# Local attention with a PReLU feed-forward: banks, first loads, visits, conversion pieces and shared sums rearranged

## The chip, the cores and the metric

The kernel runs on one core of a Trainium2 chip. The metric is the device time of one execution in microseconds (us), lower is better; several runs are timed and their median is given. The program is one launch. Its engines work side by side, each through its own list of instructions in order: TensorE (matmuls, PE in the profile; its weight loads are PEld), VectorE (DVE), ScalarE (ACT), GpSimd (POOL) and SyncE (SP), which here only issues DMA transfers. GpSimd and ScalarE can issue transfers as well.

## What is computed

Local attention over chunks of 64 positions, 8 heads of 64 columns, is followed by a feed-forward layer whose activation has a slope of its own for every hidden column where the input is negative.

```python
q_c, k_c, v_c = (a.reshape(B, H, nc, 64, D) for a in (q, k, v))      # 8 x 8 x 9 chunks, D = 64
scores = (1 / sqrt(D)) * matmul(q_c, k_c.transpose(0, 1, 2, 4, 3))
scores = scores - max(scores, axis=-1)
attn = exp(scores); attn = attn / (sum(attn, axis=-1) + 1e-9)
x = matmul(attn, v_c) -> (4608 tokens, 512)
h = x @ w_in                                                          # 512 -> 2048
g = maximum(h, 0) + alpha * minimum(h, 0)
out = g @ w_out                                                       # 2048 -> 512
```

## The kernel before

The 4608 tokens are 36 sub-blocks of 128 tokens (two chunks of 64 each); four sub-blocks are a block of 512 tokens, nine blocks in all. Float32 products are made of three passes of rounded matmuls: every operand is split into a high part (a copy on ACT) and a low part (a subtraction on DVE).

**Blocks 0 to 2 (plain).** The list `steps` has 48 steps, numbered `n`. One step is one 128-column slice `f` of the hidden layer for one block: `ffn_in` (L317, 12 matmuls of 512 columns into a bank of `ps_h`, of which there are two), `prelu` (L307 and L308 on ACT, L309 on DVE), the split into `gh` and `gl` (L329 on ACT, L330 on DVE), and one or two steps later `ffn_out` through `second` (L341, 12 matmuls into the four banks `ps_o0` to `ps_o3`, which hold a block's results). Steps 0 to 2 are block 0, 3 to 11 block 1, 12 to 24 block 0 again, 25 to 31 block 1 again, 32 to 47 block 2. The weights of slice `f` are loaded by SP (`fetch`) and converted on DVE and ACT (`split_weight`, L130 to L138) one step after the other; the conversion of slices 2, 3 and 4 is held until the x of sub-blocks 4, 6 and 7 is made.

**Attention of sub-blocks 0 to 7 (early).** Each goes through three stages, `attend(0)` scores and softmax, `attend(1)` transposes (L248) and two copies (L255, L256), `attend(2)` values (L266) and the split into `xh` and `xl` (L298, L299). Sub-blocks 0 to 3 come before the steps; 4 to 7 are spread over the steps 0 and 1 (`beside`). `attn_psum` picks the bank: scores always use `ps_a` (two banks); the transposes and values of sub-blocks 0 to 3 use `ps_o`, those of 4 to 7 `ps_a`. All first loads are issued by SP, in the order `q0 k0 wi0 q1 k1 v0 wo0 q2 k2 v1 ...`.

**Attention from sub-block 8 on.** A `visit` makes the values of one sub-block (L278, from the transposed probabilities `pT`) and the scores of the one two further on (L200, from `q_sb` and `k_sb`, one buffer each), then the softmax, the copies of x (L303 on ACT and L304 on DVE for block 2, L294 on ACT for later blocks), and `attn_blocks`, which transposes 32 by 32 squares on DVE (L231) and has SP issue eight small transfers `pT <- t` (L238). The list `visits` says ahead of which step each of the first 14 is made; the sixth makes the values of sub-block 11, the last of block 2. `combine` (in the steps listed in `COMBINE`) prepares sums of weights on DVE for what follows and is put behind the last softmax.

**Blocks 3 to 8 (three pairs).** A pair's products are made with seven instead of eight block products (`ORDERS` gives their order). `convert` makes 14 pieces of operands of a pair from x (a subtraction L567 or L571 for eight of them, and a split, L549 and L550); for the first pair they are made during steps 40 to 47, ahead of the step's `ffn_in`. `first_product` (L593) has eight parts `j`; `second_product` (L705) runs over seven products `i`, each with eight parts `j`. Weights stream through a ring of four 512 KB buffers: when a unit is used up, `stream` has GpSimd issue the load of the one four units on (L531, `raw<-wo_a` and its like). The results are `y11`, `y12`, `y21`, `y22`; products that several results share are added by GpSimd's accumulating transfers (L712, L724, L730) of 512 KB each, and the results leave by SP (`done`, L681). In `second_product` these transfers stand at `(i, j)` = (3, 0), (3, 5) and (4, 2), and after the products 7 and 5.

The order on each engine comes from a planner. It takes the instructions in program order as priorities, raised inside `tc.high_priority`, and puts on each engine the first one that its own model of time holds ready. From step 20 on the matmuls keep their program order (`pe`). `tc.issue_after(ins)` puts what its block makes behind `ins` on that instruction's engine. The names in the profile are those of the buffers: early `q`, `k`, `v` and probabilities live in buffers called `wi` and `wo`, the y tiles in `xh` and `xl`.

Of the kernel before, what the change touches and what calls it, by code (L numbers as in the profile page):

```python
# [12 lines left out]
ALU = mybir.AluOpType  # L13
# [14 lines left out]
def tile_local_attention_prelu_ffn(  # L28
# [12 lines left out]
    nc = tc.nc  # L41
# [113 lines left out]
    def attn_load(s, parts="qkv"):  # L155
        early = s < EARLY
        if "q" in parts:
            q_sb = qs[s // 2 % 2][:, s % 2] if early else load.tile([P, H, C], F32, name="q_sb")
            kb = kbds[s % NBD] if early else load.tile([P, H, C], F32, name="k_sb")
            nc.sync.dma_start(out=q_sb, in_=qT[:, s].rearrange("p (h t) -> p h t", t=C))  # L160
            if not early:
                nc.sync.dma_start(out=kb, in_=kT[:, s].rearrange("p (h t) -> p h t", t=C))
            for c in range(2 if early else 0):
                rows = slice(c * C, (c + 1) * C)
                nc.sync.dma_start(out=kb[rows, c], in_=kT[rows, s].rearrange("p (h t) -> p h t", t=C))
            qkv[s] = [q_sb, kb, None]
        if "v" in parts:
            v_sb = vs[s // 2 % 2][:, s % 2] if early else load.tile([P, DM], F32, name="v_sb", bufs=2)
            loads.append(nc.sync.dma_start(out=v_sb, in_=v[s * P:(s + 1) * P, :]))
            qkv[s][2] = v_sb  # L170

    def attn_psum(s, n):
        if s < SPB and n:
            t = 2 * (s % 2) + n - 1
            return ps_o.tile([P, 512], F32, name=f"ps_o{t}")
        return ps_a.tile([P, 512], F32, name="ps_a")
# [134 lines left out]
    def ffn_in(x, f):  # L311
# [15 lines left out]
        with tc.high_priority(offset=HIGH):  # L327
            prelu(g, hps, f)
            nc.scalar.copy(gh, g)  # L329
            nc.vector.tensor_tensor(gl, g, f32(gh), op=ALU.subtract)  # L330
# [84 lines left out]
    attn_load(0, "q")  # L415
    fetch("wi", 0)
    attn_load(1, "q")
    attn_load(0, "v")
    fetch("wo", 0)
    attn_load(2, "q")  # L420
    attn_load(1, "v")
    attn_load(3, "q")
# [21 lines left out]
    visits = [21, 23, 25, 27, 29, 31, 33, 35, 37, 39, 41, 42, 44, 45]  # L444
# [220 lines left out]
    def second_product(g, b, operands, conversion, end):  # L665
# [11 lines left out]
        def done(ys, half, col):  # L677
            for m in range(2):
                rows = slice((2 * half + m) * P, (2 * half + m + 1) * P)
                cols = slice((b - PLAIN + col) * TB, (b - PLAIN + col + 1) * TB)  # L680
                nc.sync.dma_start(out=outT[rows, cols], in_=ys[:, m])  # L681

        kept = None
        for i in ORDERS["wo"]:
# [8 lines left out]

            shared = {(3, 0): y22, (3, 5): y21, (4, 2): y12}
            for j in range(JF):
# [14 lines left out]
                if (i, j) in shared:  # L710
                    ys = shared[i, j]
                    nc.gpsimd.dma_start(out=ys, in_=y11, accum_op=ALU.add)  # L712
                    if ys is y22:
                        done(y22, 1, 1)
                    elif ys is y12:
                        done(y12, 0, 1)
# [5 lines left out]
            elif i == 7:  # L722
                copy(y21, ps)
                nc.gpsimd.dma_start(out=y22, in_=y21)  # L724
            elif i == 2:
                add(y11, ps)
                done(y11, 0, 0)
            elif i == 5:
                copy(y12, ps)
                nc.gpsimd.dma_start(out=y22, in_=y12, accum_op=ALU.add)  # L730
            elif i == 3:
                add(y12, ps)
            elif i == 6:
                copy(y11, ps)
            else:
                add(y21, ps)
                done(y21, 1, 0)
# [8 lines left out]
    for n, (p, b, f) in enumerate(steps):  # L746
# [34 lines left out]
        if n >= len(steps) - 8:  # L781
            for _ in range(1 if len(conversion) > 10 else 0 if n < len(steps) - 3 else 4):
                if conversion:
                    conversion.pop(0)()
        pending.append((acc, ffn_in(x[b], f), f, f0, f1, b, False))

        if len(pending) > (1 if n < 20 else 2):
            second(*pending.pop(0))
    assert not combined and not conversion and not finals
# [62 lines left out]
```

## Time and profile before

| | |
|---|---|
| median of 3 runs | 864.72 us (861.14 to 866.14) |
| the profiled execution | 862.12 us, its span 860.3 us |
| instructions | 15340 |
| TensorE | busy 95%, mean granted clock 0.986 of 2.4 GHz |
| DVE, ACT, POOL | busy 78%, 63%, 23% |
| DMA | 192.39 MB, mean 224 GB/s |

The profile is of one execution. The span runs from its first to its last instruction; times in it count from the span's start. A wait in brackets is idle time of that engine, with what ended it.

### The profile page before, as it was taken

Reading aid. Unit: us, or ns where it says so; the run is one execution under the profiler, and the core shown is the slowest. Engines: PE = TensorE matmul, PEld = TensorE weight load, DVE = VectorE, ACT = ScalarE, POOL = GpSimd, SP = SyncE. Lnnn points to the kernel's source line nnn. Section 1 sums busy time; section 2 is a strip of 40 time slices with the busy share of each in tenths; the row PEclk is TensorE's granted clock in tenths of the full one; section 3 lists DMA queues with packets and bytes.
Section 4 is the critical chain, followed back from the end, with each engine's and each line's share of the span. In section 5 each row is a group of like instructions: output and inputs, shape, how many; then the busy total and the mean of one; then the engine's idle time right before and its main releaser. Section 6 shows DMA issues by size and latency. Waiting matters only on the chain.

```text
span 860.3 us, 15340 instructions
## 1 busy us (share of the span) xinstructions
PE 814.4 (95%) x5248; PEld 648.0 (75%) x5248; DVE 673.3 (78%) x1267; ACT 544.9 (63%) x1392; POOL 200.1 (23%) x324
## 2 busy tenths in 40 slices
PE   4697999999989998999989999999999999999997
PEld 4576888778767776777767877777887788888885
DVE  6769999997997987476768995776789956568874
ACT  6785666667576676487776563877765546556552
POOL 3005222224443420011111221111122221111230
PEclk9899999999999999999999999999999999999999
DMA  9618768637778676587774788877567885555686
GB/s 283 194 50 312 249 199 291 218 129 204 234 247 230 212 232 211 180 260 253 250 261 164 237 220 286 274 253 242 188 200 233 230 297 185 186 193 190 236 218 213
DMA packets 73164, 192.39 MB, mean 224 GB/s; under 512 B 11648, under 2 KB 18816, under 8 KB 72960
## 3 DMA queue, kind: packets, MB, share of 16 engines
q0 software_dynamic: 36464, 127.42, 46.2%
q1 hardware_dynamic: 36480, 63.99, 23.3%
q8 instruction: 42, 0.69, 0.3%
q14 instruction: 34, 0.28, 0.1%
q10 hardware_dynamic: 144, 0.01, 0.0%
HBM read 135.27 MB, written 42.99 MB: 207 GB/s over the span
## 4 chain that ended last, share of the span: by engine, by line
PE 69%; DMA 11%; DVE 6%; issue 4%; ACT 4%; SPq 3%; POOL 2%; DVEq 0%; POOLq 0%; ACTq 0%
PE ps_o L593 18%; PE ps_h L705 12%; PE ps_h L317 10%; PE ps_o L341 9%; PE ps_h L593 8%; PE ps_o L705 8%; DMA raw<-wo_a 3%; SPq L238 2%; DMA pT<-t 2%; ACT pr L220 1%; PE ps_a L278 1%; DMA wi_a<-raw 1%; PE ps_a L200 1%; DMA v_sb<-v 1%; DMA k_sb<-kT 1%
## 5 line engine op out<-in xcount | busy, mean ns | idle before, releaser
L317 PE MATMUL ps_h<-xh,wi 128*128 128x512 f32 x384 | 110.3, 412 | 10.9 <-DVE g L309 5.4
L341 PE MATMUL ps_o<-wo,gh 128*128 128x512 f32 x384 | 114.1, 396 | 0.0
L317 PEld LDWEIGHTS ps_h<-xh,wi 128*128 128x128 f32 x384 | 73.3, 195 | 30.0 <-DVE g L309 6.3
L341 PEld LDWEIGHTS ps_o<-wo,gh 128*128 128x128 f32 x384 | 72.3, 189 | 17.4 <-issue 0.2
L220 ACT ACTIVATE pr<-ps_a,mx 128x64 f32<-128x64 f32 x224 | 67.1, 326 | 28.7 <-DVE mx L217 28.7
L341 PE MATMUL ps_o<-wo,gl 128*128 128x512 f32 x192 | 69.0, 395 | 0.0
L593 PE MATMUL ps_o<-wi,raw 128*128 128x512 f32 x171 | 67.9, 397 | 0.3 <-ACT g L614 0.3
L593 PE MATMUL ps_o<-wo,raw 128*128 128x512 f32 x171 | 67.8, 397 | 0.0
L317 PE MATMUL ps_h<-xl,wi 128*128 128x512 f32 x192 | 54.5, 405 | 0.0
L220 ACT ACTIVATION_READ_ACCUMULATOR pr<-ps_a,mx 128x1 f32 x224 | 48.8, 218 | 0.0
L531 POOL DMA_DIRECT2D raw<-wi_a x42 | 22.4, 534 | 110.8 <-PE ps_o L593 61.6
L307 ACT ACTIVATE g<-ps_h 128x512 f32<-128x512 f32 x48 | 29.4, 613 | 29.1 <-PE ps_h L317 24.4
L307 ACT ACTIVATE wo<-gh 128x512 f32<-128x512 f32 x24 | 15.2, 634 | 51.3 <-DVE gh L616 51.3
L549 ACT CAST gh<-wi 128x512 fp32r<-128x512 f32 x48 | 29.9, 623 | 27.5 <-PE ps_o L705 13.1
L329 ACT CAST gh<-g 128x512 fp32r<-128x512 f32 x48 | 29.9, 623 | 26.1 <-DVE g L309 21.3
L317 PEld LDWEIGHTS ps_h<-xl,wi 128*128 128x128 f32 x192 | 37.1, 194 | 9.2 <-DVE xl L304 0.4
L341 PEld LDWEIGHTS ps_o<-wo,gl 128*128 128x128 f32 x192 | 36.2, 189 | 8.7
L531 POOL DMA_DIRECT2D raw<-wo_a x42 | 22.5, 535 | 86.6 <-PE ps_o L705 45.2
L309 DVE SCALAR_TENSOR_TENSOR g<-ps_h,g 128x512 f32<-128x512 f32 x48 | 32.7, 684 | 9.4 <-ACT g L308 9.2
L593 PE MATMUL ps_o<-wi,wo 128*128 128x512 f32 x99 | 39.4, 398 | 0.3 <-ACT g L614 0.3
L593 PE MATMUL ps_o<-wo,wo 128*128 128x512 f32 x99 | 39.1, 395 | 0.0
L330 DVE TENSOR_TENSOR gl<-g,gh 128x512 fp32r<-128x512 f32 x48 | 32.9, 686 | 7.8 <-ACT gh L329 6.6
(249 smaller groups left out, 2269.4 us busy)
## 6 DMA issues: line engine op xcount, KB each, us to landing
raw<-wi_a POOLq DMA_DIRECT2D x42, 512.0 KB, 4.6
raw<-wo_a POOLq DMA_DIRECT2D x42, 512.0 KB, 4.6
wi<-wi_a POOLq DMA_DIRECT2D x21, 512.0 KB, 4.7
wo<-wi_a POOLq DMA_DIRECT2D x21, 512.0 KB, 4.7
wi<-wo_a POOLq DMA_DIRECT2D x21, 512.0 KB, 4.5
wo<-wo_a POOLq DMA_DIRECT2D x21, 512.0 KB, 4.8
k_sb<-kT SPq DMA_DIRECT2D x28, 256.0 KB, 5.0
q_sb<-qT SPq DMA_DIRECT2D x28, 256.0 KB, 4.0
```

The source lines that it names most:

```text
L220: last = nc.scalar.activation(pr[:, g], one, AF.Exp, bias=mx[:, g], scale=SCALE, accum_out=sm[:, g])
L238: nc.sync.dma_start(out=pT[dst, i].rearrange("p h t -> p (h t)"), in_=tb[src, j].rearrange("p h t -> p (h t)"),)
L307: nc.scalar.activation(g, h, AF.Relu, scale=-1.0)
L309: nc.vector.scalar_tensor_tensor(g, in0=h, scalar=0.0, in1=g, op0=ALU.max, op1=ALU.subtract)
L317: pe(nc.tensor.matmul(hps, lhsT=wi[f][:, l, k * P:(k + 1) * P], rhs=xx[:, k], start=(i == 0 and k == 0), stop=(i == 2 and k == NK - 1),))
L329: nc.scalar.copy(gh, g)
L330: nc.vector.tensor_tensor(gl, g, f32(gh), op=ALU.subtract)
L341: pe(nc.tensor.matmul(o, lhsT=a[:, ts], rhs=wo[f][:, l], start=(f == first and i == 0), stop=(f == last and i == 2),))
L531: nc.gpsimd.dma_start(out=f32(t), in_=units[side][n])
L549: hi = nc.scalar.copy(t_hi, t)
L593: pe(nc.tensor.matmul(ps, lhsT=w[:, l, k * P:(k + 1) * P], rhs=xx[:, xl], start=first and at == 0, stop=at == n - 1, skip_group_check=not ...
L705: pe(nc.tensor.matmul(ps[m], lhsT=w[:, l, m * P:(m + 1) * P], rhs=xx, start=i != 6 and j == 0 and n == 0, stop=j == JF - 1 and n == 2, ski ...
```

## The change

Five things. (1) `attn_load` can take a second queue: `q0` and the second half of `k0` are issued by ACT; `q1` and `k1` go ahead of `wi0`, and `wo0` goes behind `v1`. (2) `attn_psum`: sub-blocks 4 and 5 put their transposes and values into `ps_o`, as 0 to 3 do. (3) `visits`: from the sixth on each is one step earlier. (4) The pieces of the first pair: four at steps 40 to 43 as before; of the other ten, three each at steps 45, 46 and 47, issued after `ffn_in` and, on DVE, after the split of the step before, and one after the loop. (5) `second_product`: the shared sums are ten transfers of 256 KB instead of five of 512 KB, and the results leave in 256 KB pieces as their sum is done; a table `sums` says at which `(i, j)` each is written in the program.

```diff
--- before.py
+++ after.py
@@ -152,17 +152,18 @@
     stages = {}
     pdiag = {}
 
-    def attn_load(s, parts="qkv"):
+    def attn_load(s, parts="qkv", other=None):
         early = s < EARLY
         if "q" in parts:
             q_sb = qs[s // 2 % 2][:, s % 2] if early else load.tile([P, H, C], F32, name="q_sb")
             kb = kbds[s % NBD] if early else load.tile([P, H, C], F32, name="k_sb")
-            nc.sync.dma_start(out=q_sb, in_=qT[:, s].rearrange("p (h t) -> p h t", t=C))
+            (other or nc.sync).dma_start(out=q_sb, in_=qT[:, s].rearrange("p (h t) -> p h t", t=C))
             if not early:
                 nc.sync.dma_start(out=kb, in_=kT[:, s].rearrange("p (h t) -> p h t", t=C))
             for c in range(2 if early else 0):
                 rows = slice(c * C, (c + 1) * C)
-                nc.sync.dma_start(out=kb[rows, c], in_=kT[rows, s].rearrange("p (h t) -> p h t", t=C))
+                queue = other if other and c else nc.sync
+                queue.dma_start(out=kb[rows, c], in_=kT[rows, s].rearrange("p (h t) -> p h t", t=C))
             qkv[s] = [q_sb, kb, None]
         if "v" in parts:
             v_sb = vs[s // 2 % 2][:, s % 2] if early else load.tile([P, DM], F32, name="v_sb", bufs=2)
@@ -170,7 +171,7 @@
             qkv[s][2] = v_sb
 
     def attn_psum(s, n):
-        if s < SPB and n:
+        if s < SPB + 2 and n:
             t = 2 * (s % 2) + n - 1
             return ps_o.tile([P, 512], F32, name=f"ps_o{t}")
         return ps_a.tile([P, 512], F32, name="ps_a")
@@ -327,7 +328,8 @@
         with tc.high_priority(offset=HIGH):
             prelu(g, hps, f)
             nc.scalar.copy(gh, g)
-            nc.vector.tensor_tensor(gl, g, f32(gh), op=ALU.subtract)
+            low = nc.vector.tensor_tensor(gl, g, f32(gh), op=ALU.subtract)
+        stages["split"] = stages.get("split", [])[-1:] + [low]
         return gh, gl
 
     def ffn_out(acc, g, f, first, last, end=False):
@@ -412,13 +414,13 @@
             if new is not None:
                 attn_blocks(new)
 
-    attn_load(0, "q")
+    attn_load(0, "q", nc.scalar)
+    attn_load(1, "q")
     fetch("wi", 0)
-    attn_load(1, "q")
     attn_load(0, "v")
-    fetch("wo", 0)
     attn_load(2, "q")
     attn_load(1, "v")
+    fetch("wo", 0)
     attn_load(3, "q")
     attn_load(2, "v")
     attn_load(3, "v")
@@ -441,7 +443,7 @@
             if 0 <= i - st < SPB:
                 beside[2 * i // (SPB + 2)].append((st, SPB + i - st))
 
-    visits = [21, 23, 25, 27, 29, 31, 33, 35, 37, 39, 41, 42, 44, 45]
+    visits = [21, 23, 25, 27, 29, 30, 32, 34, 36, 38, 40, 41, 43, 44]
     late = {at: (EARLY + j - 2 if j > 1 else None, EARLY + j) for j, at in enumerate(visits)}
 
     pending = []
@@ -674,11 +676,17 @@
             for m in range(2):
                 nc.scalar.copy(ys[:, m], ps[m])
 
-        def done(ys, half, col):
-            for m in range(2):
-                rows = slice((2 * half + m) * P, (2 * half + m + 1) * P)
-                cols = slice((b - PLAIN + col) * TB, (b - PLAIN + col + 1) * TB)
-                nc.sync.dma_start(out=outT[rows, cols], in_=ys[:, m])
+        def done(ys, m, half, col):
+            rows = slice((2 * half + m) * P, (2 * half + m + 1) * P)
+            cols = slice((b - PLAIN + col) * TB, (b - PLAIN + col + 1) * TB)
+            nc.sync.dma_start(out=outT[rows, cols], in_=ys[:, m])
+
+
+        sums = {
+            (2, 1): (y22, y21, 0), (2, 4): (y22, y21, 1), (6, 1): (y22, y12, 0), (6, 4): (y22, y12, 1),
+            (3, 0): (y22, y11, 0), (3, 2): (y22, y11, 1), (3, 4): (y21, y11, 0), (3, 6): (y21, y11, 1),
+            (4, 1): (y12, y11, 0), (4, 3): (y12, y11, 1),
+        }
 
         kept = None
         for i in ORDERS["wo"]:
@@ -690,8 +698,6 @@
                 ps = [bank() for _ in range(2)]
             if i == 1:
                 kept = ps
-
-            shared = {(3, 0): y22, (3, 5): y21, (4, 2): y12}
             for j in range(JF):
                 at = JF * ORDERS["wo"].index(i) + j
                 if at + AHEAD + EARLIER < 7 * JF:
@@ -707,13 +713,12 @@
                             start=i != 6 and j == 0 and n == 0, stop=j == JF - 1 and n == 2,
                             skip_group_check=i == 6,
                         ))
-                if (i, j) in shared:
-                    ys = shared[i, j]
-                    nc.gpsimd.dma_start(out=ys, in_=y11, accum_op=ALU.add)
-                    if ys is y22:
-                        done(y22, 1, 1)
-                    elif ys is y12:
-                        done(y12, 0, 1)
+                if (i, j) in sums:
+                    to, what, m = sums[i, j]
+                    op = {} if to is y22 and what is y21 else {"accum_op": ALU.add}
+                    nc.gpsimd.dma_start(out=to[:, m], in_=what[:, m], **op)
+                    if what is y11 and to is not y21:
+                        done(to, m, *((1, 1) if to is y22 else (0, 1)))
                 if conversion and j % 4 == 3:
                     with tc.issue_after(behind[1][0].ins), tc.issue_after(behind[1][1].ins):
                         conversion.pop(0)()
@@ -721,20 +726,20 @@
                 copy(y11, ps)
             elif i == 7:
                 copy(y21, ps)
-                nc.gpsimd.dma_start(out=y22, in_=y21)
             elif i == 2:
                 add(y11, ps)
-                done(y11, 0, 0)
+                for m in range(2):
+                    done(y11, m, 0, 0)
             elif i == 5:
                 copy(y12, ps)
-                nc.gpsimd.dma_start(out=y22, in_=y12, accum_op=ALU.add)
             elif i == 3:
                 add(y12, ps)
             elif i == 6:
                 copy(y11, ps)
             else:
                 add(y21, ps)
-                done(y21, 1, 0)
+                for m in range(2):
+                    done(y21, m, 1, 0)
 
     def new_raw(b):
         for n, name in enumerate(("xh", "xl")):
@@ -778,14 +783,18 @@
                 combine(*combined.pop(0), n in (23, 24, 25, 26, 32, 33, 34))
         if n == len(steps) - 8:
             ops, conversion = convert(PLAIN)
-        if n >= len(steps) - 8:
-            for _ in range(1 if len(conversion) > 10 else 0 if n < len(steps) - 3 else 4):
-                if conversion:
+        if len(steps) - 8 <= n < len(steps) - 4:
+            conversion.pop(0)()
+        pending.append((acc, ffn_in(x[b], f), f, f0, f1, b, False))
+        if n >= len(steps) - 3:
+
+            with tc.issue_after(stages["split"][0].ins):
+                for _ in range(3):
                     conversion.pop(0)()
-        pending.append((acc, ffn_in(x[b], f), f, f0, f1, b, False))
 
         if len(pending) > (1 if n < 20 else 2):
             second(*pending.pop(0))
+    conversion.pop(0)()
     assert not combined and not conversion and not finals
     for _ in range(3):
         stream()
```

## Rows read from the trace of the kernel before

**Rows 1.** Page, part 1: busy time, share of the span, number of instructions.

```profile
PE 814.4 (95%) x5248; PEld 648.0 (75%) x5248; DVE 673.3 (78%) x1267; ACT 544.9 (63%) x1392; POOL 200.1 (23%) x324
```

**Rows 2.** TensorE's waits: line, what ended them, us in total, times, longest.

```profile
PE ps_h L317 <- DVE g L309: 5.4, 2, 3.7
...
PE ps_h L705 <- DMA raw<-wo_a: 5.0, 3, 1.9
PE ps_h L317 <- ACT xh L303: 3.9, 1, 3.9
PE ps_a L248 <- DVE wo L224: 3.7, 1, 3.7
```

**Rows 3.** Stretches: length, busy us (instructions) by engine, PEclk, DMA share, GB/s.

```profile
0.00:20.00 20.00, 9.85 (x88) 8.04 (x88) 12.84 (x31) 11.67 (x53) 8.38 (x20) 1.00 0.93 283
20.00:40.00 20.00, 12.92 (x115) 9.49 (x114) 13.90 (x32) 17.27 (x68) 0.00 (x0) 0.83 0.73 227
...
70.00:100.00 30.00, 28.25 (x118) 22.50 (x118) 29.35 (x61) 17.68 (x30) 15.45 (x21) 0.97 0.86 299
...
238.00:248.00 10.00, 6.28 (x20) 4.77 (x21) 9.39 (x21) 7.32 (x25) 5.57 (x8) 0.83 0.64 226
```

**Rows 4.** Timeline of the start: start, us, engine, line, operation [idle before, by].

```profile
1.19 1.20 SPq L165 DMA_DIRECT2D wo<-kT  x2
5.41 1.98 PE L186 MATMUL ps_a<-wo,wo 128*64 128x128 f32 x16 [5.41 <-DMA wo<-kT]
8.38 0.67 DVE L216 TENSOR_REDUCE mx<-ps_a 128x8 f32<-128x512 f32 x1
31.44 0.58 ACT L256 COPY wi<-ps_o 64x512 f32<-64x512 f32 x1
31.71 0.45 PE L248 MATMUL ps_a<-ident,wo 128*128 128x128 f32 x1 [3.66 <-DVE wo L224]
36.29 1.68 PE L266 MATMUL ps_o<-wi,wi 128*64 128x128 f32 x14
68.68 3.51 PE L317 MATMUL ps_h<-xh,wi 128*128 128x512 f32 x8 [1.38 <-ACT xh L298]
```

**Rows 5.** Timeline around the fifth and sixth visits, three engines.

```profile
214.88 6.17 SPq L238 DMA_DIRECT2D pT<-t  x8
218.85 0.69 PE L200 MATMUL ps_a<-k_sb,q_sb 64*64 64x64 f32 x32 [2.02 <-DMA k_sb<-kT]
240.98 0.69 ACT L303 CAST xh<-ps_a 128x256 fp32r<-128x256 f32 x2
```

**Rows 6.** Chain that ended last, pieces: start us, us, what.

```profile
241.72 4.65 PE ps_h L317 x12
246.37 2.80 PE ps_o L341 x12
...
342.19 5.49 PE ps_h L317 x12
...
506.62 1.20 POOL xh L712
507.86 9.80 DMA raw<-wo_a
517.79 12.93 PE ps_h L705 x48
...
686.78 11.32 PE ps_h L705 x48
```

**Rows 7.** DMA issues of the whole span: count, KB each, median us to landing.

```profile
raw<-wo_a POOLq DMA_DIRECT2D x42, 512.0 KB, 4.6
...
k_sb<-kT SPq DMA_DIRECT2D x28, 256.0 KB, 5.0
...
wo_a<-wo POOLq DMA_DIRECT2D x24, 256.0 KB, 3.4
```

**Rows 8.** Timeline of DVE ahead of step 47.

```profile
341.45 1.28 DVE L309 SCALAR_TENSOR_TENSOR g<-ps_h,g 128x512 f32<-128x512 f32 x2
```

## What I expect of the change

> **What bounds the kernel now.** I read the page's busy line first, then TensorE's waits by cause, then the table of stretches, then the timeline and the chain around each wait found. TensorE is busy 95% of the span [rows 1], so time is lost where it isn't, and TensorE's waits say where: the causes are few and large, one wait of 3.7 us for DVE at L309, one of 3.9 us for ACT's copy at L303, three of together 5.0 us for `raw<-wo_a`, and the start's waits for loads and for DVE at L224 [rows 2]. The stretches show the start: of the first 20 us TensorE works 9.85, of the next 20 us 12.92, at a granted clock of 0.83 [rows 3]. From 70 to 100 us DVE is busy 29.35 of 30 us, so what the start gives TensorE must also be given to DVE. A long wait costs twice: after it the matmuls run for some time at the lower level of 1.2 GHz (the stretch from 238 to 248 us has a mean clock of 0.83 [rows 3]; the pace is priced below). The change aims at four of these places. I take them one by one; each term is measured against the profiled execution, 862.12 us with a span of 860.3.
>
> **1. The start (first loads, banks of sub-blocks 4 and 5).** The first matmul waits for the second half of `k` until 5.41 [rows 4]. Moving `q` and this half to ACT's queue lets SP issue them one transfer earlier, and ACT has nothing else to do: SP's issues of `k` alone run from 1.19 to 2.39 [rows 4], behind that of `q`; on two queues the last of them ends one issue of 0.6 us sooner, so some 0.6 us. Then the first softmax starts late for another reason: its maximum on DVE runs at 8.38 although the scores ended at 7.39 (5.41 + 1.98), because the first weight landed first. The DMA engines are 0.93 busy in these 20 us at 283 GB/s, so the order of the loads is their timing: putting sub-block 1 ahead of the 512 KB of `wi0` moves the weight by about 1.8 us (0.5 MB at 283 GB/s) and takes it out of DVE's way. Together 1.6 us (0.6 and 1.0). ACT is busy 17.27 of the next 20 us, so that this carries over to 31 us.
> The banks: sub-blocks 4 to 7 share two `ps_a` banks for scores, transposes and values, and each waits for the one before. At 31.71 TensorE comes back after 3.66 us, and then runs the transposes of 4 and the scores of 5 in turn, at the low clock; sub-block 3's values, whose operand was copied at 31.44 + 0.58 = 32.02, start only at 36.29 [rows 4]. With the scores of 5 in a bank of their own they fill the idle time before 31.71, and 36.29 could be 32.1: 4.2 us at most. I take 3 of them, because the transposes of 4 still wait for their softmax, and 0.4 us for the later waits up to 68.68, where block 1's first step starts after 1.38 us [rows 4]. In all 5.0 us; the ends are 1.5 (the loads alone) and 8.0 (all of 1.6 + 4.2, and some 2 us from the waits before 68.68). The cover that decides: DVE's weight conversion after 70 us. The weights of steps 4 and 5 are tied to sub-blocks 6 and 7 and so move with them; if they didn't, TensorE would give the gain back in the steps that use them. A new wait is possible too: block 0's results need bank `ps_o3` after sub-block 5's values have been read. Sub-block 5 moves forward by more than step 0 does, so I cost it at nothing; uncovered it costs about the 0.7 us of one DVE pass (the first maximum took 0.67 [rows 4]).
>
> **2. Visits one step earlier from the sixth on.** Step 32 needs the x of sub-block 11. ACT copies it at 240.98, behind a softmax [rows 5]; TensorE waits 3.9 us [rows 2], then 12 matmuls take 4.65 us where the next 12 take 2.80 [rows 6]: 1.85 us, together 5.75. One step earlier (5.6 us: 12 matmuls of 2.80 twice) the copy would end near 236, before step 32 wants it. What is late next: visits 29 and 30 now follow each other. Visit 29 already waits 2.02 us for its `k` [rows 5], since SP first spent 6.17 us issuing eight `pT` transfers; the `k` of visit 30 may be issued only after visit 29's scores, and has one step, 5.6 us, where a `k` takes 5.0 us to land [rows 7] plus SP's queue. I expect a wait of about 2 us there or at visit 32, whose `pT` has three steps where it had four. So 5.75 less 2.25 is 3.5 us; the ends are 5.75 and nothing.
>
> **3. Next-pair pieces at steps 45 to 47.** Ten pieces of the conversion sit ahead of the prelu of steps 45 and 46: two L309 run back to back at 341.45 [rows 8], although their products were ready long before. TensorE waits 3.7 us and then takes 5.49 us for 12 matmuls, 2.69 above 2.80 [rows 2, 6]: 6.4 us. The change issues the pieces behind the step's products, in threes, each after the split of the step before, and the last visit is a step earlier. Ten pieces are 18 DVE passes of 0.64 us (two took 1.28 [rows 8]), 11.5 us; from step 45 to the next stage TensorE has eight groups of 12 matmuls, 22.4 us, so they fit. I take 6.0 us; the low end is 3, if the pieces, now later, delay the first sums of the next stage.
>
> **4. Sums in 256 KB.** The load that TensorE waits for is issued right behind two 512 KB sums and lands after 9.80 us [rows 6]; its kind takes 4.6 us in the median [rows 7]. It is wanted 8.0 us after its issue (517.79 less the 1.9 waited, less 507.86). Three such waits of 5.0 us in total [rows 2], and at 517.79 the slow pace: 48 matmuls in 12.93 us, against 11.32 us at 686.78 [rows 6], 1.6 us: 6.6 us in all. Two sums cost the load 5.2 us, so 256 KB cost 1.3. But the sum written at (3, 5) is already issued ahead of the load of (3, 2), at 506.62 [rows 6]: the planner issues what is ready, and all four halves are ready once `y11` is copied. So perhaps one or two of the four slip behind that load, 1.3 to 2.6 us where 1.7 are needed on average, and the loads behind it inherit them. I take half, 3.5 us; the ends are 6.6 and a loss of 1.5 (five more issues per pair on GpSimd's queue, which stand ahead of loads, and nothing shifted).
> A transfer of half the size is not half as long: a 256 KB store took 3.4 us from issue to landing where a 512 KB load took 4.6 [rows 7]. If the halves queue without overlap, four of them hold the load longer than two wholes; that is rival C. The Trainium skill ("DMA: Bandwidth & Descriptors", section "Anatomy of one DMA") gives every transfer a fixed cost of about 2.0 us and advises against small ones, which speaks for C; the rows, 1.2 us between the two sizes, lean the same way, but show single landings and not a queue that is full.
>
> **Sum.** 5.0 + 3.5 + 6.0 + 3.5 = 18.0 us. 862.1 less 18.0 is 844.1; the median of the runs shown lies 2.6 above the profiled one, and so 846.7 is forecast.
>
> **Rivals.** A: everything goes, 8.0 + 5.75 + 6.4 + 6.6 = 26.8 us, 838. For it: DVE and ACT have the room outside the start; against it, DVE is nearly full up to 100 us. B: the transfers stay in the way, so that the change doesn't do what it says in parts 2 and 4: the planner sends all four halves together, and step 32's wait moves to visits 30 and 32. Then 5.0 + 6.0 = 11.0 us, 853.7. C: a half costs what a whole does, and four hold the load by 10.4 us instead of 5.2: three waits grow by 5.2, 15.6 us lost against 14.5 won (5.0 + 3.5 + 6.0), 866. D, the slower one: from visit 30 on `k` is late at every visit, because eight `pT` issues (6.17 us), the issue of `v` and `q`, and the landing (5.0 us) exceed the 12.5 us from visit to visit (two steps of 5.6 and the visit's own 1.3). It decides when SP's other issues hold `k` up by 1.3 us or more each time. Nine visits with the 2.02 us seen once, and 1.85 us of slow pace after each, are 34.8 us against 14.5 won: 885. Against it: the spacing of the visits is the old one apart from one pair, and only one of them waited 2 us.
>
> **How the numbers follow.** Forecast 0.56, A 0.12, B 0.20, C 0.05, D 0.07. What a measurement can tell from no change is 0.5%, 4.3 us. Faster by more than that: the forecast, A and most of B, 0.86; within it: the rest of B and C, 0.06; slower: 0.08. From 836 (A, less the runs' spread of 2.5 us) to 858 (B with its start at the low end, and half a wait more) lies over 0.8.
>
> **What would show it.** Right: the first scores before 5 us; no wait of over 3 us near 28 to 32 us; block 1's first step near 63; no wait for L303 ahead of step 32 and none for L309 ahead of step 47; the wait for `raw<-wo_a` under 1 us each. Wrong: waits for `k_sb` or `pT` in several visits, L309 late in the pair's first stage, TensorE idle for weights in the steps after 70 us, or the load behind the sums still landing after 9 us.

## The result and the profile after

The changed kernel takes 855.25 us in the median (852.42 to 856.47), the kernel before 864.16 in the same comparison: a ratio of 0.9895 with a 95% interval of 0.9856 to 0.9934, so 8.9 us less, between 5.7 and 12.4. The profiled execution took 854.61 us with a span of 852.8. The forecast was 846.7, with a range of 836 to 858. The sign and the range held. The likeliest case did not: the time is that of rival B (853.7), and so is the mechanism. What held the forecast is its range, 22 us wide, and not its sum: 18.0 us were forecast and 8.9 measured. Two signs that the prediction named for being wrong came with it: `k_sb` late in several visits, and the load behind the sums landing after more than 9 us.

The page's busy line of the changed kernel stands against [rows 1]; PE is busy 5.4 us less with the same number of matmuls, and the mean granted clock is 0.990 instead of 0.986, so fewer of them ran at the low clock:

```profile
PE 809.0 (95%) x5248; PEld 645.0 (76%) x5248; DVE 672.2 (79%) x1267; ACT 544.6 (64%) x1392; POOL 213.7 (25%) x339
```

TensorE's waits of the changed kernel (line, what ended them, us in total, times, longest), against [rows 2]:

```profile
PE ps_h L711 <- DMA raw<-wo_a: 6.0, 3, 2.7
...
PE ps_a L201 <- DMA k_sb<-kT: 4.3, 3, 2.3
PE ps_h L318 <- DVE g L310: 4.0, 3, 2.1
PE ps_a L279 <- issue: 3.2, 1, 3.2
```

Read it by what is missing and what is new. The 3.9 us for ACT's copy (L303, now L304), the 3.66 at the start and the 3.7 ahead of step 47 are gone. The sums' wait, which should have shrunk, has grown from 5.0 to 6.0. Three waits have grown or are new: the one for `k_sb` (2.6 before), one of 2.1 us for DVE's L310 in the late visits, and one of 3.2 us ahead of a visit's values (L279).

The stretches of the changed kernel against [rows 3] (length, busy us and instructions by engine, PEclk, DMA share, GB/s):

```profile
70.00:100.00 30.00, 28.31 (x121) 22.57 (x122) 26.18 (x54) 16.98 (x30) 9.25 (x13) 1.00 0.89 297
...
238.00:248.00 10.00, 10.00 (x55) 7.83 (x57) 9.71 (x23) 6.50 (x25) 2.90 (x4) 1.00 0.71 240
```

From 238 to 248 us TensorE now works all 10 us at full clock where it worked 6.28 at 0.83. From 70 to 100 DVE is busy 26.18 us instead of 29.35, and in the 30 us before that 27.28 instead of 21.76: the weight conversion did move forward with sub-blocks 6 and 7.

To see where the time went, take the first matmul of a step, of the next-pair stage's first product, and the span's end, in the two timelines. The changed kernel's against before's: step 28 at 204.81 (5.64 earlier), step 44 at 319.86 (0.49 later), the first product at 349.14 (8.25 earlier), the end at 852.83 (7.52 earlier). So the start wins 5.6, the visits lose 6.1 by step 44, the pieces win 8.7 with the last visits, and the sums lose 0.7. Part of the 6.1 is no loss: at step 44 the changed kernel has one visit more behind it. At step 45, where both have made the same visits, it is 1.51 earlier (325.56 against 327.07), so that the visits lose 4.1. The experiments split this further; all are set out in one table behind them.

### The profile page after: what moved, and what is told of

Same layout as the page of the kernel before. It is cut to its first block, busy times and chain, and to the rows that moved or that the text cites. A ratio compares the mean times of both kernels' runs of the same rounds, so it can differ in the third digit from the quotient of the medians.

```text
span 852.8 us, 15379 instructions
## 1 busy us (share of the span) xinstructions
PE 809.0 (95%) x5248; PEld 645.0 (76%) x5248; DVE 672.2 (79%) x1267; ACT 544.6 (64%) x1392; POOL 213.7 (25%) x339
## 4 chain that ended last, share of the span: by engine, by line
PE 75%; DMA 11%; ACT 5%; DVE 4%; issue 3%; POOL 2%; SPq 0%; DVEq 0%; ACTq 0%; POOLq 0%
PE ps_o L595 17%; PE ps_h L318 13%; PE ps_h L711 12%; PE ps_o L343 11%; PE ps_o L711 10%; PE ps_h L595 8%; DMA raw<-wo_a 4%; DMA k_sb<-kT 2%; PE ps_a L279 2%; DMA raw<-w_in 1%; ACT pr L221 1%; PE ps_a L201 1%; DMA wi_a<-raw 1%; DMA wi<-kT 1%; DMA wo<-v 1%
## 5 line engine op out<-in xcount | busy, mean ns | idle before, releaser
L318 PE MATMUL ps_h<-xh,wi 128*128 128x512 f32 x384 | 106.7, 401 | 4.6 <-DVE g L310 4.0
L318 PEld LDWEIGHTS ps_h<-xh,wi 128*128 128x128 f32 x384 | 71.1, 189 | 22.7 <-DVE g L310 5.0
L221 ACT ACTIVATE pr<-ps_a,mx 128x64 f32<-128x64 f32 x224 | 67.2, 327 | 30.1 <-DVE mx L218 30.0
L221 ACT ACTIVATION_READ_ACCUMULATOR pr<-ps_a,mx 128x1 f32 x224 | 49.0, 219 | 0.0
L533 POOL DMA_DIRECT2D raw<-wo_a x42 | 26.2, 625 | 81.6 <-PE ps_o L711 37.7
L308 ACT ACTIVATE g<-ps_h 128x512 f32<-128x512 f32 x48 | 29.5, 615 | 18.4 <-PE ps_h L318 12.4
L310 DVE SCALAR_TENSOR_TENSOR g<-ps_h,g 128x512 f32<-128x512 f32 x48 | 32.6, 684 | 7.4 <-ACT g L309 7.2
L595 PEld LDWEIGHTS ps_o<-wi,raw 128*128 128x128 f32 x171 | 32.1, 188 | 8.2 <-ACT g L616 0.7
```

What stands on the lines that cost most here:

```text
L221: last = nc.scalar.activation(pr[:, g], one, AF.Exp, bias=mx[:, g], scale=SCALE, accum_out=sm[:, g])
L308: nc.scalar.activation(g, h, AF.Relu, scale=-1.0)
L310: nc.vector.scalar_tensor_tensor(g, in0=h, scalar=0.0, in1=g, op0=ALU.max, op1=ALU.subtract)
L318: pe(nc.tensor.matmul(hps, lhsT=wi[f][:, l, k * P:(k + 1) * P], rhs=xx[:, k], start=(i == 0 and k == 0), stop=(i == 2 and k == NK - 1),))
L533: nc.gpsimd.dma_start(out=f32(t), in_=units[side][n])
L595: pe(nc.tensor.matmul(ps, lhsT=w[:, l, k * P:(k + 1) * P], rhs=xx[:, xl], start=first and at == 0, stop=at == n - 1, skip_group_check=not ...
```

## The experiments

**Visits undone.**

```diff
-    visits = [21, 23, 25, 27, 29, 30, 32, 34, 36, 38, 40, 41, 43, 44]
+    visits = [21, 23, 25, 27, 29, 31, 33, 35, 37, 39, 41, 42, 44, 45]
```

> The changed kernel with the old list of visits (the sixth at step 31, the last at 45); all else as changed. Theory 1 (the earlier visits cost about 4 us between steps 29 and 45: a wait of 3.7 us for banks at visit 30 in place of the one ahead of step 32, then waits for k of 2.3, 0.5 and 1.4 us and one of 2.1 us for L310): these waits go, the wait ahead of step 32 comes back with 3.9 us and its slow pace, step 45 starts about 5.6 us earlier than in the kernel before (1.5 in the changed one), and the time is some 4 us under the changed kernel, near 851 us. Rival (the pieces need the last visit at step 44): the wait for L310 ahead of step 47 comes back with about 3.7 us and slow pace, 6 us in all, and the time is 857 us or more.

853.25 us, ratio 0.9880 [0.9839, 0.9921]. TensorE's waits of this kernel show the exchange:

```profile
PE ps_h L318 <- ACT xh L304: 4.0, 1, 4.0
PE ps_a L201 <- DMA k_sb<-kT: 3.6, 1, 3.6
```

The old wait ahead of step 32 is back, the wait ahead of visit 30's values and the L310 wait are gone, and one late `k` (at visit 45) stands for three. The total is not worse than with the earlier visits; the two intervals overlap. The pieces work with the old visits too.

**Sums undone.** The three shared sums as 512 KB transfers at their old places; all else as changed.

> The changed kernel with the old shared sums: five transfers of 512 KB per pair. Theory 1 (the four halves are all sent ahead of the weight load, so the halves won nothing and cost 1 us more of waiting): the three waits for raw<-wo_a go from 6.0 us back to about 5.0, and the time stays within 2 us of the changed kernel, 853 to 855 us. Rival (halves are worth the 3.5 us forecast, and the profile of the changed kernel only shows an unlucky run): the waits grow and the time is 857 us or more.

850.73 us, ratio 0.9827 [0.9770, 0.9884]; the waits for `raw<-wo_a` are 4.4 us, in place of 6.0. The quartered schedule wins nothing over the old one; that it loses is not shown by these times, whose intervals overlap.

**The halves held behind loads.** `stages["load"]` is the latest weight load:

```diff
+                    with tc.issue_after(stages["load"].ins):
                         nc.gpsimd.dma_start(out=to[:, m], in_=what[:, m], **op)
```

> The changed kernel, where each 256 KB sum is held on GpSimd's queue behind the weight load that the program issues ahead of it, so that loads and halves alternate as the program is written. Theory 1 (what counts is how many bytes of sums stand ahead of the load): the load behind the sums lands in about 6 us where it took 9 to 10, the three waits of together 6.0 us fall below 2 us, and with their slow pace the time falls by 3 to 6 us against the changed kernel, to about 850. Rival (the DMA engines are full there, so that the bytes count and not their order): the waits stay at 4 to 6 us, only later, and the time stays at 855.

844.97 us, ratio 0.9789 [0.9747, 0.9831], clear of both the kernel before and the changed one. GpSimd's timeline of the changed kernel (start, us, line, transfer, idle before) shows what this undoes:

```profile
496.81 0.88 POOL L719 DMA_DIRECT2D xl<-xh  x1 [2.20 <-ACT xh L677]
497.37 0.87 POOL L533 DMA_DIRECT2D wo<-wo_a  x1
497.90 1.22 POOL L719 DMA_DIRECT2D xh<-xh  x1
498.46 1.56 POOL L719 DMA_DIRECT2D xl<-xh  x1
499.01 1.88 POOL L719 DMA_DIRECT2D xh<-xh  x1
499.62 1.84 POOL L533 DMA_DIRECT2D raw<-wo_a  x1
```

All four halves (L719), written at steps (3, 0), (3, 2), (3, 4) and (3, 6), stand ahead of the load at 499.62. Its landing is in the chain that ended last of the changed kernel, in each of the three pairs, and in the last pair the matmuls behind it run slowly (12.72 us for 48, against 11.31):

```profile
499.62 9.40 DMA raw<-wo_a
509.16 11.31 PE ps_h L711 x48
...
667.13 9.70 DMA raw<-wo_a
...
824.91 10.96 DMA raw<-wo_a
836.01 12.72 PE ps_h L711 x48
```

In the kernel with the halves held, at most one stands behind each load, and TensorE's waits no longer name `raw<-wo_a`:

```profile
498.72 0.54 POOL L533 DMA_DIRECT2D raw<-wo_a  x1 [1.29 <-PE ps_o L711]
499.25 0.91 POOL L720 DMA_DIRECT2D xl<-xh  x1
501.45 0.54 POOL L533 DMA_DIRECT2D raw<-wo_a  x1 [1.29 <-PE ps_o L711]
501.98 0.91 POOL L720 DMA_DIRECT2D xh<-xh  x1
```

From the first product to the end this kernel gains 7.1 us on before, a little over the whole 6.6 us that part 4 had priced. Sums of 512 KB held in the same way were not tried, so what the halving adds to the holding is open.

**The start alone, and its two halves.** The kernel before with both parts of the start; with the loads alone; with the banks alone (one line, `if s < SPB + 2 and n:`).

> The kernel before with the start alone changed: first loads on two queues and in the new order, and the results' banks for sub-blocks 4 and 5. Theory 1 (the start gives 5.6 us and keeps them): step 3 starts 5.6 us earlier than in the kernel before, so does step 28 and the end, and the time is 5 to 6 us under the kernel before, near 858.5. Rival (DVE, full from 70 to 200 us, or the wait ahead of step 32 takes it back): the end comes at most 3 us earlier.

> The kernel before with the new order of the first loads and the two queues alone; the banks of sub-blocks 4 and 5 as before. With both parts of the start the step checkpoints of 13 to 28 stood 5.6 to 8.4 us ahead. Theory (my split of 1.6 and 3.4): they stand 1 to 3 us ahead here, and the wait of 3.66 us ahead of 31.71 stays; one time of about 861. Rival: the loads carry most of it and the banks little; then 4 us or more ahead, and 857 or less.

> The kernel before with the banks of sub-blocks 4 and 5 alone; the first loads in their old order on one queue. With both parts the steps from 13 to 28 stood 5.6 to 8.4 us ahead, with the loads alone 0.3. Theory (the banks carry the start): 5 to 8 us ahead here, the wait of 3.7 us ahead of 31.7 gone, step 3 near 63, the time 854 to 858. Rival 1 (my split): 3 to 4 us ahead, about 860. Rival 2: the banks need the loads' new order as well, since sub-block 5's scores can only fill the idle time if q and k are there; then under 2 us ahead, 861 or more.

Together: 852.98 us, ratio 0.9874 [0.9825, 0.9923], which is as much as all five parts of the change gain (0.9895). Loads alone: 862.74 in a single execution. Banks alone: 860.28, ratio 0.9978 [0.9947, 1.0009]. At step 28 they stand 8.36, 0.29 and 3.02 us ahead of before. So the banks alone give about what my split had for them (rival 1, 3.4), the loads alone less than their 1.6, and the two together 8.36 where their sum is 3.31: neither half explains the start by itself. TensorE's timeline with the loads alone still has the transposes and scores in turn in two banks from 31.09 on, so earlier operands change nothing there:

```profile
31.09 0.45 PE L249 MATMUL ps_a<-ident,wo 128*128 128x128 f32 x1 [2.17 <-DVE wo L225]
31.47 0.69 PE L187 MATMUL ps_a<-wi,wo 128*64 128x128 f32 x2
```

With the banks alone the scores of 5 fill that place, and step 4 is 5.60 us ahead; but between 69 and 125 us TensorE waits 3.8 us for DVE's L309, where before waits 1.7, and the lead shrinks to 3.0 by step 13. With both it waits 0.7 (1.9 in the changed kernel), and the ten profiles of kernels with the whole start keep their lead from step 4 to step 13, 6.1 and 6.5 us in the mean:

```profile
PE ps_h L317 <- DVE g L309: 3.8, 3, 1.7
```

DVE was late there, but not for being full: from 70 to 100 us it is busy 24.56 us with the banks alone, where before has 29.35. It stood idle for a weight. SP issued that load behind all four stores of a block's results, it took 12.2 us to land, and DVE's conversion waited for ACT, which waited for the load:

```profile
69.42 1.27 SPq L118 DMA_DIRECT2D more<-w_out  x1
81.71 0.66 ACT L130 ACTIVATE t<-more 128x512 f32<-128x512 f32 x1 [5.93 <-DMA more<-w_out]
82.40 0.43 DVE L131 TENSOR_SCALAR t<-t 128x512 f32<-128x512 f32 x1 [5.44 <-ACT t L130]
```

In the start with both parts the same load goes out behind two of the four stores and lands after 8.2 us:

```profile
66.03 1.11 SPq L118 DMA_DIRECT2D more<-w_out  x1
74.97 0.43 DVE L131 TENSOR_SCALAR t<-t 128x512 f32<-128x512 f32 x1 [0.76 <-ACT t L130]
```

In the changed kernel DVE waits 2.70 us at this place. These are single profiles; that the new order of the first loads is what brings this weight forward was not tried by itself.

**The pieces alone.** The kernel before with the pieces moved and nothing else.

> The kernel before with the moved pieces of the next pair alone. Theory: the wait of 3.7 us ahead of step 47 and the slow matmuls behind it go, and 3 to 5 us stay gained at the first product of the pair; about 859. Rival 1 (my sum): 6.0 us, about 857. Rival 2: the pieces only move their wait into the pair's first products, the end is that of before within 1 us; about 863.

862.36 us, ratio 0.9985 [0.9961, 1.0008]. The wait ahead of step 47 goes, but a late `k` (2.18 us at visit 45) takes part of it back; 2.7 us are left in the profile. Alone it is no difference that this measurement can tell.

**`k` and `q` on ACT's queue.** The changed kernel with the two loads of each later visit issued by ACT.

> The changed kernel with the q and k of each later visit issued on ACT's queue instead of SP's, so that they no longer stand behind eight issues of pT. Theory (k is late because of SP's queue): the waits for k_sb of 4.3 us in three places shrink to under 1.5 us and step 45 comes 3 to 5 us earlier against the changed kernel; about 851. Rival 1: k is held by the DMA engines, or by the tile it is written to, and the waits stay; about 855. Rival 2: the issues stand on ACT ahead of the softmax and copies and wait there for the old scores, so that ACT's copies come late; waits for ACT appear in their place, 857 or more.

857.95 us, ratio 0.9936 [0.9908, 0.9963]: no faster than the changed kernel (the intervals overlap). TensorE's waits of this kernel name `k_sb` no more, and name ACT instead:

```profile
PE ps_a L279 <- issue: 4.9, 1, 4.9
PE ps_o L343 <- ACT more L372: 3.7, 1, 3.7
```

Its ACT timeline shows the exchange: behind the two issues ACT stands idle for 4.76 us, and the copy that TensorE waits for comes after that.

```profile
252.73 0.34 ACTq L160 DMA_DIRECT2D q_sb<-qT  x1
253.16 0.71 ACTq L162 DMA_DIRECT2D k_sb<-kT  x1
258.04 1.07 ACT L372 COPY more<-ps_o 128x512 f32<-128x512 f32 x2 [4.76 <-DMA q_sb<-qT]
```

So SP's queue is one half of why `k` was late. At the visit ahead of step 36 SP issued `k` 5.85 us after the scores before it had ended (248.96 and 254.81), ACT 1.19 us after them (251.97 and 253.16). The other half stays on either queue: that `k` landed 8.37 us after its issue by SP and 8.0 us after its issue by ACT, while the DMA engines were busy throughout (share 1.09 and 1.03). This half is rival 1. The vanished wait alone doesn't tell the two apart, since TensorE also came to these scores 6 us later (269.33 for 263.31). ACT is no better place for the issues (rival 2).

**One weight sum later, and all of them earlier.** Two attempts on the visits' waits: the changed kernel with the weight product of step 28 moved to 29, and the kernel with the halves held with those from 30 on a step earlier.

> The changed kernel with the sums of one weight product moved from step 28 to step 29, so that DVE has one pass group less ahead of visit 29's copies of x. Theory (visit 30 waits for a bank that visit 29's softmax and copies hold, because DVE is behind): the wait of 3.25 and 0.44 us ahead of visit 30's values shrinks below 2 us, about 853 in one look. Rival: the bank is held by the order of work alone (two visits a step apart need both banks in turn); the wait stays at 3 us or more, 855.

> The changed kernel with alternating sums, and the weight products' sums from step 30 on moved one step earlier, so that they stand to the visits as they did before the change. With the changed visits eight of them fall on a visit's own step (30, 32, 34, 36, 38, 40, 41, 43), with the old ones three did (31, 37, 41). Theory (DVE's sums stand ahead of the visits' softmax, so pT and k come late): the waits for k_sb and for DVE's L310 between 255 and 330 us shrink from some 5 us to under 2 us, 841 to 843; the wait at visit 30 stays. Rival: the waits come from the visits' own transfers; they stay, and the time is 844 to 846, or worse since DVE has more to do round visits 29 and 30.

852.57 us in a single execution, with 3.76 and 0.35 us ahead of visit 30's values: as in the changed kernel. And 848.11 us, ratio 0.9823 [0.9783, 0.9863], with 3.5 us for `k` and 2.7 for L310 between 255 and 330 us, where the kernel with the halves held has 3.9 for `k` and none for L310. Neither took the waits away; the planner put DVE's sums ahead of the softmax in the first all the same. That the weight sums make `k` and `pT` late is not borne out.

**Old visits with the halves held, and `x` copied ahead of the softmax.** The second kernel differs from the first by this:

```diff
+            if old is not None:
+                attn_x(old, xo)
             if new is not None:
                 attn_softmax(new, sc3)
-            if old is not None:
-                attn_x(old, xo)
```

> The changed kernel with the visits at their old steps and the four half sums each issued behind a later load, so that sums and loads alternate. Alone, the old visits gave 853.25 against 855.25, and the alternation 844.97. Theory (the visits cost some 2 us, independently of the sums): the waits for raw<-wo_a stay away, the wait of 4 us ahead of step 32 is back, the wait and the late k of visits 30 to 43 are gone; 841 to 844. Rival: the earlier visits are worth something (my 3.5 us of part 2) and the run with the old visits was lucky; 846 to 849.

> As the kernel with the old visits and alternating sums, and besides in each visit the copies of x are put ahead of the softmax in the order in which the work is given out. Theory (step 32 waits because ACT copies x of sub-block 11 behind the eight exponentials of a softmax): the wait for L304 ahead of step 32 shrinks from 4 us to under 1.5 us and the slow matmuls behind it go, about 4 to 5 us less than the kernel with the old visits, 838 to 840. Rival: the copy is late because the planner has other work ahead of it, or the softmax, now later, makes pT and with it k late; then the wait stays over 3 us or comes back as waits for k_sb and pT, 843 or more.

847.21 us, ratio 0.9823 [0.9768, 0.9879], and 845.35 us, ratio 0.9798 [0.9741, 0.9854]. In the timeline of the first, the copy for step 32 stands behind the last exponential (L221) and TensorE resumes with it, after 3.80 us and at the low clock:

```profile
232.19 0.35 ACT L221 ACTIVATE pr<-ps_a,mx 128x64 f32<-128x64 f32 x1
232.96 0.70 ACT L304 CAST xh<-ps_a 128x256 fp32r<-128x256 f32 x2
233.71 2.07 PE L318 MATMUL ps_h<-xh,wi 128*128 128x512 f32 x4 [3.80 <-ACT xh L304]
```

In the second it runs 4.6 us ahead of the first exponential, and step 32's matmuls, at 231.16, wait for nothing:

```profile
227.54 0.64 ACT L304 CAST xh<-ps_a 128x256 fp32r<-128x256 f32 x2
231.16 1.09 PE L318 MATMUL ps_h<-xh,wi 128*128 128x512 f32 x4
232.10 0.31 ACT L221 ACTIVATE pr<-ps_a,mx 128x64 f32<-128x64 f32 x1
```

That removes the wait at its cause without a step moved. It did not bring the 4 to 5 us that I expected: waits for `k_sb` are 3.7 us in the second and 2.0 in the first, as its rival said. The two medians don't tell the kernels apart, nor either from the 844.97 of the kernel with the halves held and the changed visits; that the first, too, lies where its rival put it says little for the same reason.

**All profiles side by side** (us against the profile of before; minus is earlier). The columns are the change up to step 28, from there to step 44, from there to the next-pair stage's first product, and from there to the end:

| kernel | to step 28 | to step 44 | to first product | to the end |
|---|---|---|---|---|
| changed | -5.6 | +6.1 | -8.7 | +0.7 |
| sums undone | -7.0 | +8.0 | -7.8 | +0.6 |
| halves held | -5.6 | +5.3 | -8.7 | -7.1 |
| one weight sum later | -6.7 | +5.5 | -8.7 | +0.4 |
| `k` on ACT | -5.6 | +10.3 | -8.5 | +2.9 |
| halves held, weight sums earlier | -6.6 | +8.1 | -7.3 | -7.6 |
| visits undone | -7.3 | -1.8 | -2.1 | +0.6 |
| halves held, old visits | -7.0 | +0.1 | -2.7 | -7.5 |
| the same, `x` first | -4.9 | -2.1 | -5.5 | -6.2 |
| start alone | -8.4 | -0.4 | +0.6 | -0.8 |
| loads alone | -0.3 | +0.7 | +0.5 | -0.3 |
| banks alone | -3.0 | +2.2 | -1.0 | -1.9 |
| pieces alone | +0.9 | +1.0 | -3.5 | -1.1 |

One profile scatters by some 2 us in each column, so the terms below are means, and differences of 1 us between them say little.

## Why the prediction was right, and where its steps were not

**Part 1, forecast -5.0: right in place, too small, and its split was wrong.** The ten profiles with the whole start have -6.5 in the mean (-4.9 to -8.4, the ends were 1.5 and 8.0). Rows of the changed kernel that answer [rows 4]:

```profile
5.05 1.98 PE L187 MATMUL ps_a<-wo,wo 128*64 128x128 f32 x16 [5.05 <-DMA wo<-kT]
7.06 0.69 DVE L217 TENSOR_REDUCE mx<-ps_a 128x8 f32<-128x512 f32 x1 [4.91 <-PE ps_a L187]
33.66 1.97 PE L267 MATMUL ps_o<-wi,wi 128*64 128x128 f32 x16 [0.91 <-ACT wi L257]
63.12 2.02 PE L318 MATMUL ps_h<-xh,wi 128*128 128x512 f32 x8
```

The maximum stands 1.3 us earlier (forecast 1.0), sub-block 3's values 2.6 us (forecast 3 of 4.2), and block 1's first step is at 63.12, as expected. The 0.6 us on the first matmul is not to be seen: with the new loads it ran at 5.05, 5.29 and 5.98, without them at 5.41 and 5.62. The failed step is the sum itself: I added 1.6 us of loads to 3.4 of banks as if each paid alone, and the loads alone pay 0.3 (one execution). The two need one another, and not at the place where I had priced the loads: what they add to the banks shows after step 4. The cover that I had named, the weight conversion after 70 us, is the right place: with the banks alone 2.6 of 5.6 us were lost there. But it lacked a weight, which landed late, and not DVE's time.

**Part 2, forecast -3.5: nothing.** Step 32's wait and its slow matmuls went, as said. But with the new pieces the time from step 28 to the first product changes by -2.3 us in the mean of four profiles with the earlier visits and by -3.0 in three with the old ones: the earlier visits give nothing. That they cost something is not shown: the first four scatter from -3.4 to +0.2. Two steps failed. I priced "what is late next" by `k` alone and missed the banks: visit 30 needs both `ps_a` banks while visit 29's softmax and copies still read them. Timeline of the changed kernel:

```profile
211.06 0.69 PE L201 MATMUL ps_a<-k_sb,q_sb 64*64 64x64 f32 x32
215.32 0.75 DVE L217 TENSOR_REDUCE mx<-ps_a 128x4 f32<-128x256 f32 x2
219.83 0.69 ACT L304 CAST xh<-ps_a 128x256 fp32r<-128x256 f32 x2
220.27 0.42 DVE L305 TENSOR_TENSOR xl<-ps_a,xh 128x256 fp32r<-128x256 f32 x1
220.80 0.29 PE L279 MATMUL ps_a<-pT,v_sb 64*64 64x64 f32 x2 [3.25 <-issue]
221.06 0.37 DVE L305 TENSOR_TENSOR xl<-ps_a,xh 128x256 fp32r<-128x256 f32 x1
221.53 1.02 PE L279 MATMUL ps_a<-pT,v_sb 64*64 64x64 f32 x27 [0.44 <-DVE xl L305]
```

The scores end at 211.75, their maximum begins 3.6 us later, and each L305's end (220.69, 221.43) releases a bank 0.1 us ahead of the matmuls that follow. The visit's values and scores then take 1.02 and 1.16 us, where 0.69 is usual, and the next 12 matmuls 3.49 against 2.80 in the chain: with the waits of 3.25 and 0.44 some 5.2 us, about what step 32's wait had cost. Second, `k` was late as in rival D, but three times and not at each visit: 2.33, 0.51 and 1.42 us. The first of them landed 8.37 us after its issue (chain: `254.81 8.37 DMA k_sb<-kT`), where 5.0 was my price, and the kernel with `k` on ACT shows that only the late issue is SP's doing. I could have seen the long landing before: the row of 6.17 us in [rows 5] that I blamed for the late `k` of visit 29 stands behind its issue, at 211.06; the eight issues ahead of it began at 202.82 and took 6.61, and `k` then took some 7.7 us to land. Why DVE served the maximum of visit 29 so late is argued from the order of its work only, since neither kernel with moved weight sums changed it. It is as late with the visits undone (scores to 210.30, maximum at 214.21), where no visit follows at once and nothing waits for it.

**Part 3, forecast -6.0: right, but about 4.** From step 28 to the first product, three kernels with old visits and old pieces stand at +0.9 in the mean, the three with old visits and new pieces at -3.0: 3.9 us, inside the ends of 3 and 6.4. The mis-sized term is the wait of 3.7 with its slow matmuls, taken as always there: where a late `k` at visit 45 holds TensorE for 5.3 us (start alone), DVE catches up, and the old pieces cost only 1.0 us of it. This gain rests on the profiles: in the times of the pieces alone (0.9985) it is not seen.

**Part 4, forecast -3.5: a loss of 1 to 2.** From the first product to the end, four profiles with the quartered sums have +1.2 in the mean, five with the old ones -0.7. The difference is 1.9, near the loss of 1.5 that I had as the end. The two kernels that differ in the sums alone, changed and sums undone, don't show it in that column (+0.7 and +0.6); they and all others show it in TensorE's wait for `raw<-wo_a`, 5.7 to 6.4 us in the four with the quartered sums and 4.3 to 5.0 in the six with the old ones. The step that failed is the half that I took: I had noted that the planner issues what is ready, and still let one or two halves slip behind the load. None did, in any of the three pairs. The halves' landing, in the list of DMA issues of the changed kernel (count, KB, median us):

```profile
xl<-xh POOLq DMA_DIRECT2D x18, 256.0 KB, 6.0
...
xl<-xl POOLq DMA_DIRECT2D x6, 256.0 KB, 4.9
...
xh<-xh POOLq DMA_DIRECT2D x6, 256.0 KB, 8.4
```

and of the wholes in the kernel before:

```profile
xl<-xh POOLq DMA_DIRECT2D x9, 512.0 KB, 6.8
...
xl<-xl POOLq DMA_DIRECT2D x3, 512.0 KB, 6.6
...
xh<-xh POOLq DMA_DIRECT2D x3, 512.0 KB, 8.8
```

A half lands 0.4 to 1.7 us sooner than a whole, nowhere in half the time. The fixed cost of about 2.0 us per transfer issued by GpSimd, which the Trainium skill states ("DMA: Bandwidth & Descriptors", section "Anatomy of one DMA"), points the same way; these are medians of transfers that queue, and no run here shows that cost by itself. Yet rival C fell: the load behind four halves landed after 9.4 to 11.0 us, behind two wholes after 9.25 to 9.80, and not 5.2 us later. What decides is how much is queued ahead of the load, and the held halves show it.

**Sum.** -6.5, +0.8, -3.9 and +1.9 make -7.7 us, against -7.5 in the profile. My 18.0 was too much by parts 2 and 4 almost alone, which rival B had at nothing; that its time fits within 2 us is in part luck, since its start was 1.5 us too small, its pieces 2.1 too large, and the sums cost what it had at nothing. The chance of 0.20 for it was too small: that the planner sends what is ready could be read from the rows of before, and that a visit needs both banks from its program. Of the four parts only the start shows in the times themselves: alone it is no slower than the whole change, so that no gain of the other three together can be seen there.

## What to carry to other kernels

Where a planner issues what is ready, the place at which a transfer is written orders nothing: tie it behind the load that it must not delay, which here was worth about 8 us of 855 in the profiles (and 10.3 in the medians, 6.0 with the old visits). Before a step is moved, list everything that its predecessor still holds when it starts (banks, queue, buffers), and price the longest hold, not the one that the last profile happened to show. And ask whether two edits that feed one another can pay at all one by one, before adding their gains, and time each part alone: here one of them gave as much as the whole.

## What the hardware showed that was not expected

Halving an accumulating transfer from 512 to 256 KB shortened its landing by 0.4 to 1.7 us only (8.8 to 8.4, 6.8 to 6.0, 6.6 to 4.9), and a load behind 1 MB of them landed after 9.4 to 11.0 us with four of them, and after 9.25 to 9.80 with two. ACT stood idle for 4.76 us behind two DMA issues of its own (252.73 and 253.16); the profile puts that down to the transfer of `q`, and what held it was not tried further. A 256 KB `k` that usually lands in 4.4 to 5.0 us took 8.37 us when issued by SP and 8.0 by ACT while the DMA engines were busy throughout, so that the queue made no difference to the landing. The same code at the same place scatters: the lead at step 28 differed by 3.5 us between ten profiles of one start, and it did so already at step 13, up to which their programs are the same.
